# Running the 128-row matmuls of an attention and feed-forward kernel as pairs of 64-row passes, in a new order

## The chip, the cores and the metric

The kernel runs on one core of a Trainium2 chip. The metric is the device time of one execution in microseconds (us).

In the profile PE is TensorE's matmul, PEld its weight load, DVE is VectorE, ACT is ScalarE, POOL is GpSimd and SP is SyncE. To *evict* a bank is to copy a finished result out of it, by ACT or DVE; until then the program writes no new result into it. L328 is a line of the source; nearly all matmuls go through one helper and so have one line.

## The reference

```python
x = A_x                                   # 1 x 2048 x 448
xn = layernorm(x)
# A: 16 query heads, 8 key/value heads of 256, the last 512 keys of the cache
q = (xn @ wq)                             # 448 -> 16 * 256
p = softmax(q @ k.T * 256 ** -0.5)        # 2048 x 512 for each head, no mask
s = (p @ v) @ wo                          # 16 * 256 -> 448
# B
g = silu((gelu(xn @ w_gate) * (xn @ w_up)) @ w_down)    # 448 -> 1792 -> 448
out = x + s * g
```

The queries are taken in four chunks of 512, so attention is 64 (chunk, head) steps. I call such a step a head.

## The kernel before

The query projection and gate/up contract over 448 rows, which is seven times 64. They already run as *pairs*: one matmul on rows 0 to 63 and one on rows 64 to 127, at the same time, into two banks (a bank takes one result of up to 128x512). In a first phase each half of the array feeds one bank; in a second phase they swap banks. A second phase waits until the first has landed (`before`). A *unit* is one head's query projection into one pair of banks.

```python
def group(units, lo, hi, start, stop, phases=(0, 1)):
    ...                                             # cut: loop over phases and units
                for u, j in ((0, ph), (1, 1 - ph)):
                    rows = slice(R * u, R * u + R)  # R = 64
                    ...
            before = [last_row[b][0]] if b in last_row and last_row[b][1] != ph else []
```

The rest runs as full 128-row matmuls. Scores (S) go into four banks AB, P V into two of four banks BB, alternating by head. P V follows two heads behind, because its operand `pT` comes from a DMA transpose of the normalized probabilities `pn`.

```python
def s_mm(m):
    for t4 in range(4):
        b = AB[t4]
        mms([... for e in range(2)], ..., (b_ps[b],))   # two matmuls of 128x512
        # ACT: exp of the bank to p32, with its row sum; DVE: reciprocal, normalize to pn
        # after each second tile: DMA transpose pn -> pT

def pv(m):
    for e in range(2):
        b = BB[m % 2 * 2 + e]
        mms([... for j in range(NJ)], ..., (b_ps[b],))  # four matmuls
        # evict to oT: e == 0 by ACT, e == 1 by DVE

for m in range(NS):
    if m in groups:                                     # heads 0, 8, 20, 32, 44, 56
        for i in range(m, groups[groups.index(m) + 1], 2):
            q_group(i, (cur, nxt)[i // 2 % 2])          # cur is AB, nxt is BB: two units each
        ...
    s_mm(m)
    if m < LAG:                                         # LAG = 2
        down(NQC - LAG + m, nxt)
        ...
    if len(late) == LAG:
        pv(late.pop(0))
    ...                                                 # cut: output projection at the end of a chunk
    late.append(m)
```

A block of query projections and a block of heads alternate. Twelve query slots hold the evicted `qT`, so five query blocks follow the first.

The softmax here doesn't subtract the row's maximum and nothing guards it: scores larger than these inputs give would overflow.

Of the kernel before, what the change touches and what calls it, by code (L numbers as in the profile page):

```python
# [164 lines left out]
def bass_recurrent_scan__sliding_block_cached__geglu_ffn__prompt_kernel(  # L165
# [31 lines left out]
    CUT = D - P  # L197
    HG = 8
    NG = Hq // HG
    QS = 12  # L200

    es = ExitStack()
    with es:
# [3 lines left out]
        def place(name, shape, dt, at=None):  # L207
            size = {BF16: 2, F32: 4}[dt]
            for n in shape[1:]:
                size *= n  # L210
            size = (size + 31) // 32 * 32
            if at is None:
                at = base[0]
                base[0] += size
            assert at + size <= nc.sbuf_usable_end, (name, at + size, nc.sbuf_usable_end)
            return nc.alloc_sbuf_tensor_at(name, list(shape), dt, offset=at), at, at + size

        def sbuf_bufs(at, size, n):
            return [K.buf(at + i * size, size) for i in range(n)]
# [67 lines left out]
        b_gl = sbuf_bufs(a, QC * 2, NGL)  # L287


        NPT, NPN, NP32 = 3, 3, 3  # L290
        pT, a, at = place("pT", [P, NPT, 2, 2, NJ, P], BF16, at=rf)
        b_pT = [sbuf_bufs(a + i * QC * NJ * 2, QC * NJ, 2) for i in range(NPT)]
        pn, a, at = place("pn", [P, NPN, 2, W], BF16, at=at)
        b_pn = sbuf_bufs(a, 2 * W * 2, NPN)
        p32, a, at = place("p32", [P, NP32, W], F32, at=at)
# [1 line left out]
        assert at <= b_wgu.hi  # L297
        oT, a, at = place("oT", [P, NCO, QC], BF16, at=b_wgu.hi)
        b_oT = sbuf_bufs(a, QC * 2, NCO)
        qT, a, at = place("qT", [P, QS, 2, QC], BF16, at=b_gl[0].lo - (QS - HG) * 2 * QC * 2)  # L300
        assert b_oT[-1].hi <= a
        b_qT = [[K.buf(a + (h * 2 + e) * QC * 2, QC * 2) for e in range(2)] for h in range(QS)]

        pall = [es.enter_context(nc.psum_tensor("bank%d" % i, [P, 1024], F32)) for i in range(4)]
        bank = [pall[i // 2][:, (i % 2) * 512:(i % 2) * 512 + 512] for i in range(8)]
# [3 lines left out]
        out_view = out.rearrange("b (t p) d -> p (b t) d", p=P)  # L309

        def qs(n):
            return QS - 1 - n % QS


        def dma(q, o, i, reads=(), writes=()):
# [2 lines left out]
        def dma_t(o, i, reads=(), writes=()):  # L318
            K.op("sp", lambda e, o=o, i=i: e.dma_start_transpose(o, i), reads, writes, dma=True)

        def act(o, i, func, reads, writes, scale=1.0):
            K.op("act", lambda e, o=o, i=i: e.activation(o, i, func, scale=scale), reads, writes)  # L322

        def mms(lst, reads, writes, after=()):
            def fn(e):
                ins = None
                for (o, l, r, st, sp) in lst:
                    ins = e.matmul(o, lhsT=l, rhs=r, start=st, stop=sp)  # L328
                return ins
            return K.op("pe", fn, reads, writes, after=after)  # L330
# [107 lines left out]

        last_row = {}

        def warm(n, b, w):
            def fn(e):
                ins = None
                for i in range(n):
                    ins = e.matmul(bank[b][:, 0:w], lhsT=gl[:, 0, 0:P], rhs=gl[:, 0, 0:w], start=True, stop=True)
                return ins
            last_row[b] = (K.op("pe", fn, (b_gl[0],), b_ps[b:b + 2]), None)
# [39 lines left out]
        def bk(pairs, j):  # L487
            return pairs[j // 2] + j % 2

        def gu_evac(n, b):  # L490
# [3 lines left out]
            K.op("dve", lambda e: e.tensor_tensor(actT[:, c % 2, f, :], bank[b + 1], gl[:, s, :], ALU.mult),  # L494
                 (b_ps[b + 1], b_gl[s]), (b_actT[c % 2][f],))

        def down(c, pairs):
            for t4 in range(4):
                t = c * 4 + t4
                b = bk(pairs, t4)  # L500
                mms([(bank[b][:, 0:D], actT[:, c % 2, f, t4 * P:(t4 + 1) * P], wd[:, f, :], f == 0, f == NF - 1)
                     for f in range(NF)], [b_wd] + b_actT[c % 2], (b_ps[b],))
                s = t % 2
                act(tmp[:, s, :], bank[b][:, 0:D], ACT.Tanh, (b_ps[b],), b_tmp[s], scale=0.5)
                K.op("dve", lambda e, t=t, b=b, s=s: e.scalar_tensor_tensor(
                    out=g2[:, t, :], in0=tmp[:, s, :], scalar=1.0, in1=bank[b][:, 0:D],
                    op0=ALU.add, op1=ALU.mult), b_tmp[s] + [b_ps[b]], (b_g2[t],))

        def ln_first(t):
            ln_stats(t)  # L510
# [23 lines left out]
        ln_first(1)  # L534
        ln_second(0)
        ln_tp_pe(0, ((0, 6), (1, 4)))
        warm(2, 2, QC // 2)
        ln_second(1, "act")
        HEAD, PH = (0, 1, 2), (0, 2, 4)
        T = ((None, 6),)  # L540
# [91 lines left out]

        AB, BB = [], []

        def s_mm(m):
            s, g = qs(m), m % Hq // 2
            for t4 in range(4):
                b = AB[t4]
                mms([(bank[b], qT[:, s, e, t4 * P:(t4 + 1) * P], kT[:, g, e, :], e == 0, e == 1) for e in range(2)],
                    [b_kT[g]] + b_qT[s], (b_ps[b],))  # L640
                n = m * 4 + t4
                r, z, y, x = n % NRS, n % NP32, n // 2 % NPN, n // 4 % NPT
                K.op("act", lambda e, b=b, r=r, z=z: e.activation(  # L643
                    p32[:, z, :], bank[b], ACT.Exp, scale=att_scale, accum_out=rsum[:, r:r + 1]),
                    (b_ps[b],), (b_p32[z], b_rsum[r]))
                K.op("dve", lambda e, r=r: e.reciprocal(rden[:, r:r + 1], rsum[:, r:r + 1]), (b_rsum[r],), (b_rden[r],))  # L646
                K.op("dve", lambda e, r=r, z=z, y=y, t=t4 % 2: e.tensor_scalar(  # L647
                    pn[:, y, t, :], p32[:, z, :], rden[:, r:r + 1], None, op0=ALU.mult),
                    (b_p32[z], b_rden[r]), (b_pn[y],))
                if t4 % 2 == 1:  # L650
                    dma_t(pT[:, x, t4 // 2, :, :, :].rearrange("p t j q -> p (t j) q"),
                          pn[:, y, :, :].rearrange("p t k -> p (t k)"), (b_pn[y],), (b_pT[x][t4 // 2],))

        def pv(m):
            h = m % Hq
            g, x = h // 2, m % NPT
            for e in range(2):
                b = BB[m % 2 * 2 + e]
                mms([(bank[b].rearrange("p (t q) -> p t q", q=P), va[:, g, j, e * P:(e + 1) * P],
                      pT[:, x, :, :, j, :].rearrange("p a t q -> p (a t) q"), j == 0, j == NJ - 1)  # L660
                     for j in range(NJ)], [b_va[g]] + b_pT[x], (b_ps[b],))
                i = 2 * h + e
                if e == 0:
                    act(oT[:, i, :], bank[b], ACT.Copy, (b_ps[b],), (b_oT[i],))
                else:
                    K.op("dve", lambda v, i=i, b=b: v.tensor_copy(oT[:, i, :], bank[b]), (b_ps[b],), (b_oT[i],))  # L666

        def wo_mm(t4, b, lo, hi, c0=0, c1=D):
            ch = list(range(lo, hi))
            mms([(bank[b][:, c0:c1], oT[:, i, t4 * P:(t4 + 1) * P], wo[:, i, c0:c1], i == 0, i == NCO - 1)  # L670
                 for i in ch],
                [b_oT[i] for i in ch] + [b_wo[p] for p in sorted({i // 8 for i in ch})],
                (b_ps[b],))

        def wo_fin(c, t4, b, c0=0, c1=D):
            t = c * 4 + t4
# [10 lines left out]
            if t + NXR < NT:  # L687
                dma("pool", xr[:, t % NXR, :], x_view[:, t + NXR, :], (), (b_xr[t % NXR],))

        LAG = 2  # L690
        late = []
        NS = NQC * Hq
        groups = [0, HG] + list(range(HG + QS, NS, QS)) + [NS]

        act(tmp[:, 1, 0:1], nhalf[:, :], ACT.Exp, (b_nhalf,), (b_tmp[1][0],))
        K.reuse([b for y in b_qT[QS - HG:] for b in y])
        AB.extend(bk(cur, j) for j in range(4))
        BB.extend(bk(nxt, j) for j in range(4))
        for m in range(NS):
            if m in groups:  # L700
                for i in range(m, groups[groups.index(m) + 1], 2):
                    q_group(i, (cur, nxt)[i // 2 % 2])
                if m == 0:
                    K.reuse([b for x in b_pT for b in x] + b_pn + b_p32)
            s_mm(m)
            if m < LAG:
                down(NQC - LAG + m, nxt)
                if m == LAG - 1:
                    K.reuse(b_oT + [b for y in b_qT[:QS - HG] for b in y])
            if len(late) == LAG:  # L710
                pv(late.pop(0))
            if m > Hq and m % Hq == LAG - 1:
                c = m // Hq - 1
                for t4 in range(4):
                    if t4 == 0:
                        wo_mm(0, BB[0], 0, NCO - 2)
                        wo_mm(0, BB[0], NCO - 2, NCO)
                    else:
                        wo_mm(t4, BB[t4], 0, NCO)
                    wo_fin(c, t4, BB[t4])  # L720
            late.append(m)
        c = NQC - 1
        LATE = NCO - 2 * (LAG + 1)
        wo_mm(0, AB[0], 0, LATE)
        pv(late.pop(0))
        pv(late.pop(0))
        wo_mm(1, AB[1], 0, LATE)
        wo_mm(0, AB[0], LATE, NCO)
        wo_fin(c, 0, AB[0])
        wo_mm(1, AB[1], LATE, NCO)  # L730
        wo_fin(c, 1, AB[1])
        wo_mm(2, AB[2], 0, NCO)
        wo_fin(c, 2, AB[2])
        for i in range(2):
            b = (AB[3], BB[0])[i]
            lo, hi = ((0, CUT), (CUT, D))[i]
            wo_mm(3, b, 0, NCO, lo, hi)
            wo_fin(c, 3, b, lo, hi)
# [55 lines left out]
```

## Time and profile before

556.44 us, median of 4 runs (556.19 to 556.74).

| | before |
|---|---|
| PE busy, share of the span | 547.6 us, 99% |
| PE's share of the chain that ended last | 98% |
| start to start, 128x512 full matmul | 216 ns |
| start to start, 64x512 pair | 216 ns |
| start to start, 128x448 full matmul | 189 ns |

From the page: the span, the busy time of each engine, the granted clock in 40 slices (9 is full), and the chain of waits by engine.

```profile
span 554.7 us, 9719 instructions
...
PE 547.6 (99%) x3603; PEld 261.2 (47%) x3628; DVE 317.2 (57%) x817; ACT 273.6 (49%) x727; POOL 32.7 (6%) x64
...
PEclk9999999999999999999999999999999999999999
...
PE 98%; DMA 1%; issue 0%; DVE 0%; SPq 0%; ACT 0%
```

The last column of the groups below is the idle time of the engine just before their instructions. Behind the matmuls of P V and of the queries there is none. The busy time of one matmul (379 or 376 ns) is longer than its start-to-start distance, because matmuls are pipelined; it must not be multiplied by a count.

```profile
L328 PE MATMUL bank<-pT,va 128*128 128x512 bf16 x512 | 120.8, 379 | 0.0
L328 PE MATMUL bank<-kT,qT 128*128 128x512 bf16 x487 | 117.8, 379 | 2.0 <-ACT qT L322 1.0
L328 PE MATMUL bank<-xnT,wq 64*128 64x512 bf16 x768 | 94.4, 376 | 0.0
```

So costs are read from starts. This is the timeline of PE (start, duration, engine, line, tile, number of instructions) at the end of a query block.

```profile
272.43 0.38 PE L328 MATMUL bank<-xnT,wqr 64*128 64x512 bf16 x2
272.65 1.46 PE L328 MATMUL bank<-xnT,wq 64*128 64x512 bf16 x12
274.27 1.67 PE L328 MATMUL bank<-kT,qT 128*128 128x512 bf16 x7 [0.16 <-ACT qT L322]
275.78 1.89 PE L328 MATMUL bank<-pT,va 128*128 128x512 bf16 x8
277.50 1.89 PE L328 MATMUL bank<-kT,qT 128*128 128x512 bf16 x8
279.23 1.89 PE L328 MATMUL bank<-pT,va 128*128 128x512 bf16 x8
```

One pair takes 272.65 - 272.43 = 0.22 us. Eight full matmuls take 279.23 - 277.50 = 1.73 us, 0.216 each. (Of the first score block one record is missing, "x7".) And this is a start of a query block:

```profile
253.98 1.89 PE L328 MATMUL bank<-pT,va 128*128 128x512 bf16 x8
255.80 0.82 PE L328 MATMUL bank<-xnT,wq 64*128 64x512 bf16 x6
```

Here eight full matmuls take 1.82 us to the next start, not 1.73: 0.1 us is lost between full matmuls and pairs. The Trainium skill, "TensorEngine Tiling (Array Packing)", section Tiling Modes, says that changing the tiling mode drains the TensorE. The trace shows the loss, not the drain itself: about 0.09 to 0.11 us at each of 15 such edges (six from queries to scores, five from P V to queries, four around the down projections), 1.5 us in all. At the six edges from queries to scores the first score matmul has no record ("x7" above; 487 records stand beside 512 weight loads), so there one distance of 216 ns is taken off as well.

### The profile page before, as it was taken

To read this page: it belongs to the slowest core of one execution; us is meant where nothing else is said; L and a number is where in the kernel's file an instruction comes from. 1 tells how busy PE (TensorE), PEld (TensorE's weight loads), DVE (VectorE), ACT (ScalarE), POOL (GpSimd) and SP (SyncE) were. 2 spreads that over 40 slices of the span, in tenths; PEclk is the share of its full clock that TensorE was granted. 3 is DMA by queue.
4 is the path that set the end of the run, shared out by engine and by line. 5 is a ranking of instruction groups with operands and counts; after the bars stand their busy time and mean duration, and the time that the engine had idled before them with its cause. 6 is when DMAs were issued, how large, how long until landed. Compare 5 with 4: busy or idle time off the path is not lost.

```text
span 554.7 us, 9719 instructions
## 1 busy us (share of the span) xinstructions
PE 547.6 (99%) x3603; PEld 261.2 (47%) x3628; DVE 317.2 (57%) x817; ACT 273.6 (49%) x727; POOL 32.7 (6%) x64
## 2 busy tenths in 40 slices
PE   8999999999999999999999999999999999999997
PEld 5554444444544444554444444544444454444455
DVE  6673734443385588326588745258747625858722
ACT  5432324353485588205588635058747505758600
POOL 1120580000000000000000000000000000000000
PEclk9999999999999999999999999999999999999999
DMA  9540399901156077413086803157704713618601
GB/s 295 115 141 9 79 302 307 213 1 39 38 134 96 5 149 157 88 35 92 1 153 152 153 1 77 33 94 164 146 11 95 134 34 90 153 19 153 153 8 34
DMA packets 163599, 57.63 MB, mean 104 GB/s; under 512 B 151456, under 2 KB 160672, under 8 KB 163552
## 3 DMA queue, kind: packets, MB, share of 16 engines
q1 hardware_dynamic: 159488, 45.16, 38.8%
q0 software_dynamic: 3296, 11.27, 6.7%
q8 instruction: 29, 0.48, 0.4%
q10 hardware_dynamic: 768, 0.57, 0.3%
q14 instruction: 18, 0.15, 0.1%
HBM read 17.92 MB, written 1.84 MB: 36 GB/s over the span
## 4 chain that ended last, share of the span: by engine, by line
PE 98%; DMA 1%; issue 0%; DVE 0%; SPq 0%; ACT 0%
PE bank L328 98%; DMA x<-in_A_x_dram 1%; SPq L316 0%; DVE stats L375 0%; ACT xnT L322 0%; DVE tmp L681 0%; ACT ve L391 0%; DVE ofin L684 0%; PE bank L426 0%; DVE mv L378 0%
## 5 line engine op out<-in xcount | busy, mean ns | idle before, releaser
L643 ACT ACTIVATE p<-bank 128x512 f32<-128x512 f32 x256 | 149.2, 597 | 103.3 <-PE bank L328 101.4
L647 DVE TENSOR_SCALAR pn<-p,rden 128x512 bf16<-128x512 f32 x256 | 124.6, 487 | 14.4 <-DMA pT<-pn 5.4
L328 PE MATMUL bank<-pT,va 128*128 128x512 bf16 x512 | 120.8, 379 | 0.0
L328 PE MATMUL bank<-kT,qT 128*128 128x512 bf16 x487 | 117.8, 379 | 2.0 <-ACT qT L322 1.0
L328 PE MATMUL bank<-wo,oT 128*128 128x448 bf16 (+2 forms) x544 | 97.7, 341 | 0.0
L328 PE MATMUL bank<-xnT,wq 64*128 64x512 bf16 x768 | 94.4, 376 | 0.0
L328 PE MATMUL bank<-xnT,wgu 64*128 64x512 bf16 (+2 forms) x768 | 83.9, 350 | 0.4 <-ACT xnT L322 0.4
L328 PEld LDWEIGHTS bank<-pT,va 128*128 128x128 bf16 x512 | 50.1, 98 | 60.4 <-DMA pT<-pn 0.2
L328 PEld LDWEIGHTS bank<-kT,qT 128*128 128x128 bf16 x512 | 49.6, 98 | 61.3 <-issue 2.5
L328 PEld LDWEIGHTS bank<-wo,oT 128*128 128x128 bf16 x544 | 52.0, 98 | 45.5
L630 DVE CAST qT<-bank 128x512 bf16<-128x512 f32 x64 | 42.9, 692 | 51.9 <-PE bank L328 51.9
L322 ACT ACTIVATE qT<-bank 128x512 bf16<-128x512 f32 x64 | 38.2, 597 | 60.7 <-PE bank L328 59.1
L328 PEld LDWEIGHTS bank<-xnT,wq 64*128 64x128 bf16 x768 | 36.9, 94 | 46.5 <-ACT p L643 2.1
L322 ACT ACTIVATE gl<-bank 128x512 bf16<-128x512 f32 x56 | 33.2, 597 | 49.4 <-PE bank L328 46.2
L494 DVE TENSOR_TENSOR actT<-bank,gl 128x512 bf16<-128x512 f32 x56 | 37.8, 689 | 33.4 <-PE bank L328 26.6
L328 PEld LDWEIGHTS bank<-xnT,wgu 64*128 64x128 bf16 x768 | 36.9, 94 | 37.4 <-issue 0.7
L643 ACT ACTIVATION_READ_ACCUMULATOR p<-bank 128x1 f32 x256 | 52.8, 206 | 0.0
L646 DVE RECIPROCAL rden<-rsum 128x1 f32<-128x1 f32 x256 | 40.4, 158 | 20.6 <-ACT p L643 20.0
L681 DVE SCALAR_TENSOR_TENSOR tmp<-bank,g 128x448 f32<-128x448 f32 (+2 forms) x17 | 10.1, 597 | 72.5 <-PE bank L328 72.5
L666 DVE CAST oT<-bank 128x512 bf16<-128x512 f32 x64 | 43.8, 684 | 6.9 <-PE bank L328 6.9
L328 PE MATMUL bank<-wd,actT 128*128 128x448 bf16 x224 | 43.0, 353 | 0.0
L322 ACT ACTIVATE oT<-bank 128x512 bf16<-128x512 f32 x64 | 39.1, 611 | 7.0 <-PE bank L328 7.0
(39 smaller groups left out, 182.9 us busy)
## 6 DMA issues: line engine op xcount, KB each, us to landing
wo<-in_A_wo_dram POOLq DMA_DIRECT2D x4, 896.0 KB, 19.0
wq<-in_A_wq_dram POOLq DMA_DIRECT2D x2, 1536.0 KB, 10.0
va<-in_A_v_cache_dram POOLq DMA_DIRECT2D x8, 256.0 KB, 13.9
pT<-pn SPq DMA_TRANSPOSE x128, 2.8
xr<-in_A_x_dram POOLq DMA_DIRECT2D x16, 112.0 KB, 2.3
out_dram<-ofin SPq DMA_DIRECT2D x15, 112.0 KB, 1.7
wd<-in_B_w_down_dram SPq DMA_DIRECT2D x1, 1568.0 KB, 7.6
x<-in_A_x_dram SPq DMA_DIRECT2D x2, 448.0 KB, 4.4
```

The source lines that it names most:

```text
L322: K.op("act", lambda e, o=o, i=i: e.activation(o, i, func, scale=scale), reads, writes)
L328: ins = e.matmul(o, lhsT=l, rhs=r, start=st, stop=sp)
L494: K.op("dve", lambda e: e.tensor_tensor(actT[:, c % 2, f, :], bank[b + 1], gl[:, s, :], ALU.mult), (b_ps[b + 1], b_gl[s]), (b_actT[c % 2][ ...
L630: K.op("dve", lambda v, s=s, b=b: v.tensor_copy(qT[:, s, 1, :], bank[b + 1]), (b_ps[b + 1],), (b_qT[s][1],))
L643: K.op("act", lambda e, b=b, r=r, z=z: e.activation(p32[:, z, :], bank[b], ACT.Exp, scale=att_scale, accum_out=rsum[:, r:r + 1]), (b_ps[b] ...
L646: K.op("dve", lambda e, r=r: e.reciprocal(rden[:, r:r + 1], rsum[:, r:r + 1]), (b_rsum[r],), (b_rden[r],))
L647: K.op("dve", lambda e, r=r, z=z, y=y, t=t4 % 2: e.tensor_scalar(pn[:, y, t, :], p32[:, z, :], rden[:, r:r + 1], None, op0=ALU.mult), (b_p ...
L666: K.op("dve", lambda v, i=i, b=b: v.tensor_copy(oT[:, i, :], bank[b]), (b_ps[b],), (b_oT[i],))
L681: K.op("dve", lambda e: e.scalar_tensor_tensor(out=tmp[:, s, c0:c1], in0=bank[b][:, c0:c1], scalar=0.5, in1=g2[:, t, c0:c1], op0=ALU.mult, ...
```

## The change

The intent: with all large products in 64-row pairs, TensorE needn't change its mode. A second phase must wait for the first, so other work has to stand between the two; scores of one head and P V of another are interleaved for that. P V then goes three heads behind, which needs a fourth `pT` buffer; its memory comes from four of the twelve query slots. The core of the diff:

```diff
-    QS = 12
...
-        NPT, NPN, NP32 = 3, 3, 3
+        NPT, NPN, NP32 = 4, 3, 3
...
-        def s_mm(m):
+        def s_mm(m, i, ph):
...
+            b = AB[2 * i]
+            o = mms([(bank[b + v], qT[rows, s, e, (2 * i + v) * P:(2 * i + v + 1) * P], kT[rows, g, e, :],
+                      ph == 0 and e == 0, ph == 1 and e == 1) for e in range(2) for rows, v in HV[ph]],
+                    [b_kT[g]] + b_qT[s], b_ps[b:b + 2], [first["s", i]] if ph else [])
...
-        LAG = 2
+        LAG = 3
...
-            if m in groups:
-                for i in range(m, groups[groups.index(m) + 1], 2):
-                    q_group(i, (cur, nxt)[i // 2 % 2])
+            if m % HG == 0:
+                for i in range(0, HG, 2):
+                    q_group(m + i, (cur, nxt)[i // 2 % 2])
...
-            s_mm(m)
...
+                p = late.pop(0)
+                s_mm(m, 0, 0)
+                pv(p, 0)
+                s_mm(m, 0, 1)
+                s_mm(m, 1, 0)
+                pv(p, 1)
+                s_mm(m, 1, 1)
```

Cut: the same treatment of `pv`, `down` and the output projection, a warm-up in pairs, and a new order at the very end, where the last output tiles stay full matmuls.

More of the change, by code (lines that the diff above doesn't have):

```diff
@@ L287, in bass_recurrent_scan__sliding_block_cached__geglu_ffn__prompt_kernel, with place_pT @@
         b_gl = sbuf_bufs(a, QC * 2, NGL)
-        NPT, NPN, NP32 = 3, 3, 3
-        pT, a, at = place("pT", [P, NPT, 2, 2, NJ, P], BF16, at=rf)
-        b_pT = [sbuf_bufs(a + i * QC * NJ * 2, QC * NJ, 2) for i in range(NPT)]
+        NPT, NPN, NP32 = 4, 3, 3
+        pT = [None] * NPT
+        b_pT = [None] * NPT
+        at = rf
+        def place_pT(i, at):
+            pT[i], a, at = place("pT%d" % i, [P, 2, 2, NJ, P], BF16, at=at)
+            b_pT[i] = sbuf_bufs(a, QC * NJ, 2)
+            return at
+        for i in range(NPT - 1):
+            at = place_pT(i, at)
         pn, a, at = place("pn", [P, NPN, 2, W], BF16, at=at)
@@ L299, in bass_recurrent_scan__sliding_block_cached__geglu_ffn__prompt_kernel @@
         b_oT = sbuf_bufs(a, QC * 2, NCO)
-        qT, a, at = place("qT", [P, QS, 2, QC], BF16, at=b_gl[0].lo - (QS - HG) * 2 * QC * 2)
-        assert b_oT[-1].hi <= a
-        b_qT = [[K.buf(a + (h * 2 + e) * QC * 2, QC * 2) for e in range(2)] for h in range(QS)]
+        at = place_pT(NPT - 1, at)
+        assert at <= b_gl[0].lo
+        qT, a, at = place("qT", [P, HG, 2, QC], BF16, at=b_gl[0].lo)
+        b_qT = [[K.buf(a + (h * 2 + e) * QC * 2, QC * 2) for e in range(2)] for h in range(HG)]
         pall = [es.enter_context(nc.psum_tensor("bank%d" % i, [P, 1024], F32)) for i in range(4)]
@@ L311, in qs @@
         def qs(n):
-            return QS - 1 - n % QS
+            return HG - 1 - n % HG
         def dma(q, o, i, reads=(), writes=()):
@@ L439, in bass_recurrent_scan__sliding_block_cached__geglu_ffn__prompt_kernel, with warm_pairs, fn @@
         last_row = {}
+        def warm_pairs(n, b, w):
+            def fn(e):
+                ins = None
+                for i in range(n):
+                    for u in range(2):
+                        r = slice(R * u, R * u + R)
+                        ins = e.matmul(bank[b + u][:, 0:w], lhsT=gl[r, 0, 0:P], rhs=gl[r, 0, 0:w], start=True, stop=True)
+                return ins
+            last_row[b] = (K.op("pe", fn, (b_gl[0],), b_ps[b:b + 2], after=[last_row[b][0]]), None)
         def warm(n, b, w):
@@ L495, in gu_evac, with halves @@
                  (b_ps[b + 1], b_gl[s]), (b_actT[c % 2][f],))
+        def halves():
+            return [[(slice(R * u, R * u + R), u ^ ph) for u in range(2)] for ph in range(2)]
+        HV = halves()
         def down(c, pairs):
-            for t4 in range(4):
-                t = c * 4 + t4
-                b = bk(pairs, t4)
-                mms([(bank[b][:, 0:D], actT[:, c % 2, f, t4 * P:(t4 + 1) * P], wd[:, f, :], f == 0, f == NF - 1)
-                     for f in range(NF)], [b_wd] + b_actT[c % 2], (b_ps[b],))
-                s = t % 2
-                act(tmp[:, s, :], bank[b][:, 0:D], ACT.Tanh, (b_ps[b],), b_tmp[s], scale=0.5)
-                K.op("dve", lambda e, t=t, b=b, s=s: e.scalar_tensor_tensor(
-                    out=g2[:, t, :], in0=tmp[:, s, :], scalar=1.0, in1=bank[b][:, 0:D],
-                    op0=ALU.add, op1=ALU.mult), b_tmp[s] + [b_ps[b]], (b_g2[t],))
+            first = [None, None]
+            for ph in range(2):
+                for i in range(2):
+                    b = pairs[i]
+                    o = mms([(bank[b + v][:, 0:D], actT[rows, c % 2, f, (2 * i + v) * P:(2 * i + v + 1) * P],
+                              wd[rows, f, :], ph == 0 and f == 0, ph == 1 and f == NF - 1)
+                             for f in range(NF) for rows, v in HV[ph]],
+                            [b_wd] + b_actT[c % 2], b_ps[b:b + 2], first[i:i + 1] if ph else [])
+                    first[i] = o
+                    for v in range(2 * ph):
+                        t = c * 4 + 2 * i + v
+                        s = t % 2
+                        act(tmp[:, s, :], bank[b + v][:, 0:D], ACT.Tanh, (b_ps[b + v],), b_tmp[s], scale=0.5)
+                        K.op("dve", lambda e, t=t, b=b + v, s=s: e.scalar_tensor_tensor(
+                            out=g2[:, t, :], in0=tmp[:, s, :], scalar=1.0, in1=bank[b][:, 0:D],
+                            op0=ALU.add, op1=ALU.mult), b_tmp[s] + [b_ps[b + v]], (b_g2[t],))
         def ln_first(t):
@@ L536, in bass_recurrent_scan__sliding_block_cached__geglu_ffn__prompt_kernel @@
         ln_tp_pe(0, ((0, 6), (1, 4)))
-        warm(2, 2, QC // 2)
+        warm_pairs(2, 2, QC // 2)
         ln_second(1, "act")
@@ L633, in bass_recurrent_scan__sliding_block_cached__geglu_ffn__prompt_kernel @@
         AB, BB = [], []
-        def s_mm(m):
+        first = {}
+        def s_mm(m, i, ph):
             s, g = qs(m), m % Hq // 2
-            for t4 in range(4):
-                b = AB[t4]
-                mms([(bank[b], qT[:, s, e, t4 * P:(t4 + 1) * P], kT[:, g, e, :], e == 0, e == 1) for e in range(2)],
-                    [b_kT[g]] + b_qT[s], (b_ps[b],))
-                n = m * 4 + t4
-                r, z, y, x = n % NRS, n % NP32, n // 2 % NPN, n // 4 % NPT
-                K.op("act", lambda e, b=b, r=r, z=z: e.activation(
+            b = AB[2 * i]
+            o = mms([(bank[b + v], qT[rows, s, e, (2 * i + v) * P:(2 * i + v + 1) * P], kT[rows, g, e, :],
+                      ph == 0 and e == 0, ph == 1 and e == 1) for e in range(2) for rows, v in HV[ph]],
+                    [b_kT[g]] + b_qT[s], b_ps[b:b + 2], [first["s", i]] if ph else [])
+            first["s", i] = o
+            if ph == 0:
+                return
+            y, x = (2 * m + i) % NPN, m % NPT
+            for v in range(2):
+                n = m * 4 + 2 * i + v
+                r, z = n % NRS, n % NP32
+                K.op("act", lambda e, b=b + v, r=r, z=z: e.activation(
@@ L644, in s_mm @@
                     p32[:, z, :], bank[b], ACT.Exp, scale=att_scale, accum_out=rsum[:, r:r + 1]),
-                    (b_ps[b],), (b_p32[z], b_rsum[r]))
+                    (b_ps[b + v],), (b_p32[z], b_rsum[r]))
                 K.op("dve", lambda e, r=r: e.reciprocal(rden[:, r:r + 1], rsum[:, r:r + 1]), (b_rsum[r],), (b_rden[r],))
-                K.op("dve", lambda e, r=r, z=z, y=y, t=t4 % 2: e.tensor_scalar(
-                    pn[:, y, t, :], p32[:, z, :], rden[:, r:r + 1], None, op0=ALU.mult),
+                K.op("dve", lambda e, r=r, z=z, v=v: e.tensor_scalar(
+                    pn[:, y, v, :], p32[:, z, :], rden[:, r:r + 1], None, op0=ALU.mult),
@@ L649, in s_mm, with pv @@
                     (b_p32[z], b_rden[r]), (b_pn[y],))
-                if t4 % 2 == 1:
-                    dma_t(pT[:, x, t4 // 2, :, :, :].rearrange("p t j q -> p (t j) q"),
-                          pn[:, y, :, :].rearrange("p t k -> p (t k)"), (b_pn[y],), (b_pT[x][t4 // 2],))
-        def pv(m):
+            dma_t(pT[x][:, i, :, :, :].rearrange("p t j q -> p (t j) q"),
+                  pn[:, y, :, :].rearrange("p t k -> p (t k)"), (b_pn[y],), (b_pT[x][i],))
+        def pv(m, ph):
             h = m % Hq
@@ L656, in pv @@
             g, x = h // 2, m % NPT
-            for e in range(2):
-                b = BB[m % 2 * 2 + e]
-                mms([(bank[b].rearrange("p (t q) -> p t q", q=P), va[:, g, j, e * P:(e + 1) * P],
-                      pT[:, x, :, :, j, :].rearrange("p a t q -> p (a t) q"), j == 0, j == NJ - 1)
-                     for j in range(NJ)], [b_va[g]] + b_pT[x], (b_ps[b],))
-                i = 2 * h + e
-                if e == 0:
-                    act(oT[:, i, :], bank[b], ACT.Copy, (b_ps[b],), (b_oT[i],))
-                else:
-                    K.op("dve", lambda v, i=i, b=b: v.tensor_copy(oT[:, i, :], bank[b]), (b_ps[b],), (b_oT[i],))
+            b = BB[m % 2 * 2]
@@ new lines, in pv @@
+            o = mms([(bank[b + v].rearrange("p (t q) -> p t q", q=P), va[rows, g, j, v * P:(v + 1) * P],
+                      pT[x][rows, :, :, j, :].rearrange("p a t q -> p (a t) q"), ph == 0 and j == 0,
+                      ph == 1 and j == NJ - 1) for j in range(NJ) for rows, v in HV[ph]],
+                    [b_va[g]] + b_pT[x], b_ps[b:b + 2], [first["p", m % 2]] if ph else [])
+            first["p", m % 2] = o
+            if ph == 0:
+                return
+            i = 2 * h
+            act(oT[:, i, :], bank[b], ACT.Copy, (b_ps[b],), (b_oT[i],))
@@ new lines, in pv, with wo_reads, wo_pair @@
+            K.op("dve", lambda v: v.tensor_copy(oT[:, i + 1, :], bank[b + 1]), (b_ps[b + 1],), (b_oT[i + 1],))
+        def wo_reads(ch):
+            return [b_oT[i] for i in ch] + [b_wo[p] for p in sorted({i // 8 for i in ch})]
+        def wo_pair(k, b, ph, lo, hi):
+            ch = list(range(lo, hi))
+            o = mms([(bank[b + v][:, 0:D], oT[rows, i, (2 * k + v) * P:(2 * k + v + 1) * P], wo[rows, i, :],
+                      ph == 0 and i == 0, ph == 1 and i == NCO - 1) for i in ch for rows, v in HV[ph]],
+                    wo_reads(ch), b_ps[b:b + 2], [first["w", k]] if ph else [])
+            if ph == 0:
+                first["w", k] = o
@@ L670, in wo_mm @@
             mms([(bank[b][:, c0:c1], oT[:, i, t4 * P:(t4 + 1) * P], wo[:, i, c0:c1], i == 0, i == NCO - 1)
-                 for i in ch],
-                [b_oT[i] for i in ch] + [b_wo[p] for p in sorted({i // 8 for i in ch})],
-                (b_ps[b],))
+                 for i in ch], wo_reads(ch), (b_ps[b],))
         def wo_fin(c, t4, b, c0=0, c1=D):
@@ L688, in wo_fin @@
                 dma("pool", xr[:, t % NXR, :], x_view[:, t + NXR, :], (), (b_xr[t % NXR],))
-        LAG = 2
+        LAG = 3
         late = []
         NS = NQC * Hq
-        groups = [0, HG] + list(range(HG + QS, NS, QS)) + [NS]
         act(tmp[:, 1, 0:1], nhalf[:, :], ACT.Exp, (b_nhalf,), (b_tmp[1][0],))
-        K.reuse([b for y in b_qT[QS - HG:] for b in y])
+        K.reuse([b for y in b_qT for b in y])
         AB.extend(bk(cur, j) for j in range(4))
@@ L699, in bass_recurrent_scan__sliding_block_cached__geglu_ffn__prompt_kernel @@
         for m in range(NS):
-            if m in groups:
-                for i in range(m, groups[groups.index(m) + 1], 2):
-                    q_group(i, (cur, nxt)[i // 2 % 2])
+            if m % HG == 0:
+                for i in range(0, HG, 2):
+                    q_group(m + i, (cur, nxt)[i // 2 % 2])
                 if m == 0:
-                    K.reuse([b for x in b_pT for b in x] + b_pn + b_p32)
-            s_mm(m)
-            if m < LAG:
-                down(NQC - LAG + m, nxt)
-                if m == LAG - 1:
-                    K.reuse(b_oT + [b for y in b_qT[:QS - HG] for b in y])
@@ L710, in bass_recurrent_scan__sliding_block_cached__geglu_ffn__prompt_kernel @@
-            if len(late) == LAG:
-                pv(late.pop(0))
+                    K.reuse([b for x in b_pT[:NPT - 1] for b in x] + b_pn + b_p32)
+            if len(late) == LAG:
+                p = late.pop(0)
[5 more added lines that the diff above has]
+                s_mm(m, 1, 1)
+            else:
+                for ph in range(2):
+                    s_mm(m, 0, ph)
+                    s_mm(m, 1, ph)
@@ L712, in bass_recurrent_scan__sliding_block_cached__geglu_ffn__prompt_kernel @@
+            late.append(m)
+            if m < 2:
+                down(NQC - 2 + m, nxt)
+                if m == 1:
+                    K.reuse(b_oT + b_pT[NPT - 1])
             if m > Hq and m % Hq == LAG - 1:
                 c = m // Hq - 1
-                for t4 in range(4):
-                    if t4 == 0:
-                        wo_mm(0, BB[0], 0, NCO - 2)
-                        wo_mm(0, BB[0], NCO - 2, NCO)
-                    else:
-                        wo_mm(t4, BB[t4], 0, NCO)
-                    wo_fin(c, t4, BB[t4])
@@ L721, in bass_recurrent_scan__sliding_block_cached__geglu_ffn__prompt_kernel @@
-            late.append(m)
+                wo_pair(0, BB[0], 0, 0, NCO - 2)
+                wo_pair(0, BB[0], 0, NCO - 2, NCO)
+                wo_pair(1, BB[2], 0, 0, NCO)
+                for k in range(2):
+                    wo_pair(k, BB[2 * k], 1, 0, NCO)
+                    for v in range(2):
+                        wo_fin(c, 2 * k + v, BB[2 * k + v])
         c = NQC - 1
         LATE = NCO - 2 * (LAG + 1)
-        wo_mm(0, AB[0], 0, LATE)
-        pv(late.pop(0))
-        pv(late.pop(0))
@@ L727, in bass_recurrent_scan__sliding_block_cached__geglu_ffn__prompt_kernel @@
-        wo_mm(1, AB[1], 0, LATE)
-        wo_mm(0, AB[0], LATE, NCO)
-        wo_fin(c, 0, AB[0])
-        wo_mm(1, AB[1], LATE, NCO)
-        wo_fin(c, 1, AB[1])
-        wo_mm(2, AB[2], 0, NCO)
+        wo_pair(0, AB[0], 0, 0, LATE)
+        pv(late[0], 0)
+        pv(late[1], 0)
+        pv(late[0], 1)
+        pv(late[1], 1)
+        wo_pair(0, AB[0], 1, 0, LATE - 4)
+        pv(late[2], 0)
+        wo_pair(0, AB[0], 1, LATE - 4, LATE)
+        pv(late[2], 1)
+        wo_mm(2, AB[2], 0, NCO - 2)
@@ L733, in bass_recurrent_scan__sliding_block_cached__geglu_ffn__prompt_kernel @@
+        wo_mm(2, AB[2], NCO - 2, NCO)
         wo_fin(c, 2, AB[2])
+        for t4 in (1, 0):
+            wo_mm(t4, AB[t4], LATE, NCO)
+            wo_fin(c, t4, AB[t4])
         for i in range(2):
```

## The prediction

> **Bound now.** TensorE. Part 1 of the page gives PE 547.6 us of a 554.7 us span, the chain of waits is 98% PE, the clock is full in every slice. The timeline shows the issue rate: eight 128-row score matmuls (512 columns) take 1.73 us to the next block's start, 216 ns each; nine 64-row pairs of the query projection take 1.94 us, also 216 ns a pair. Output-projection matmuls (448 columns) start 189 ns apart. A pair costs what one 128-row matmul costs, and as many columns are streamed before and after: the arithmetic gains nothing. Weight loads don't limit pairs: 128-column pairs in the head start 56 ns apart.
>
> **Removed.** Only changes of tiling mode. The Trainium skill, "TensorEngine Tiling (Array Packing)", Tiling Modes, says that a mode change drains the TensorE. This trace agrees and gives the size: a P V block followed by query pairs takes 1.82 us to the next start instead of 1.73, about 0.1 us; the down projection's edges show the same. About 15 such edges: gain 1.5 us, all critical. Nothing here can give 2%.
>
> **Added.** New order per head: S0a, PVa, S0b, S1a, PVb, S1b (0.43, 0.86, 0.43, 0.43, 0.86, 0.43 us). Two score tiles now finish at the very end of a head, with nothing behind them that leaves their banks alone.
>
> From the timeline: an eviction starts about 0.21 us after its pair's stream ends; exponentials follow each other every 0.57 us; one ends 0.69 us after its start with its accumulator read; the PE starts about 0.06 us after a releaser's end.
>
> 1. Start of a query block (7 times: heads 8 to 56). Its second unit needs the banks of the last two score tiles 0.86 us after the scores end; their second exponential ends at about 1.55 us (a P V eviction is ahead of it). Before, a 1.73 us P V stood between. Stall 0.7 us x 7 = 5 us.
> 2. End of a query block (7 times). P V of an odd head comes 0.43 us after the last query pair and needs exactly the last unit's banks, whose VectorE eviction (0.69 us) ends at 0.9 us. Before, 1.73 us of scores stood between. Stall 0.5 us x 7 = 3.6 us.
> 3. Head 3 follows head 2 without P V: 1.1 us, once.
> 4. Steady heads: the last exponential ends 1.55 to 1.6 us after the scores' end; its bank is wanted at 1.73. Slack 0.1 us, where it was over 1. Waits of pn for its transpose (six in the waits view, up to 1.1 us) now reach the PE: 0 to 5 us, 1.5 expected.
>
> ScalarE and VectorE work is unchanged, 2.8 and 3.1 us per 3.45 us head.
>
> **Sum.** 556.7 - 1.5 + 5 + 3.6 + 1.1 + 1.5 = 566.4 us, range 560.5 to 571.0. Chances: faster by over 2%: 0.01; within 2%: 0.67; slower by over 2% (above 567.8): 0.32.
>
> **What would show it.** Pairs at 216 and 189 ns; edges of 0.1 us gone; in the waits view, PE waiting for ACT p about seven times for 0.7 us and for DVE qT about seven times for 0.5 us; PE share about 97%. If 4 is right, short PE waits for ACT p within a query group.
>
> **What would make it wrong.** Steady heads that stall each time (0.1 us x 55): up to 572. Pairs faster than 216 ns would make it a gain; nothing in this trace shows that. If the waits at block edges are hidden: 555.

## The result, and the profile after

564.46 us, median of 4 runs (564.43 to 564.63): 8.0 us more. The ratio is 1.014, with a 95% interval of 1.0122 to 1.0158. Ratios in this document need not be the ratio of the medians quoted (here 1.0144).

The page of the changed kernel, same lines:

```profile
span 562.7 us, 12926 instructions
...
PE 550.9 (98%) x5310; PEld 269.3 (48%) x5310; DVE 316.2 (56%) x817; ACT 278.7 (50%) x727; POOL 32.7 (6%) x64
...
PEclk9999999999999999999999999999999999999999
...
PE 93%; ACT 4%; DVE 2%; issue 0%; ACTq 0%
```

PE's share of the chain falls from 98% to 93%, and ACT and DVE enter it. The chain in order of time (start, length, what) shows where; these are the pieces around the first query block after the start:

```profile
152.93 17.03 PE bank L336 x156
170.00 0.47 issue
170.47 1.27 ACT p L681 x4
171.79 10.77 PE bank L336 x98
182.58 1.35 DVE qT L660 x2
183.97 25.66 PE bank L336 x236
```

An exponential (`p`) holds up the start of the block, an eviction of the queries (`qT`) its end. The waits view (who waited for whom: us in total, times, longest) gives the counts:

```profile
PE bank L336 <- ACT p L681: 4.8, 8, 0.9
...
PE bank L336 <- DVE qT L660: 2.5, 7, 0.4
```

The timeline at 170 us, PE and ACT lines:

```profile
169.78 0.59 PE L336 MATMUL bank<-kT,qT 64*128 64x512 bf16 x4
169.98 0.60 ACT L330 ACTIVATE oT<-bank 128x512 bf16<-128x512 f32 x1
...
170.21 0.81 PE L336 MATMUL bank<-xnT,wq 64*128 64x512 bf16 x6
170.47 0.59 ACT L681 ACTIVATE p<-bank 128x512 f32<-128x512 f32 x1
...
170.85 0.38 PE L336 MATMUL bank<-xnT,wqr 64*128 64x512 bf16 x2
...
171.04 0.60 ACT L681 ACTIVATE p<-bank 128x512 f32<-128x512 f32 x1
...
171.52 0.21 ACT L681 ACTIVATION_READ_ACCUMULATOR p<-bank 128x1 f32 x1
171.78 0.33 PEld L336 LDWEIGHTS bank<-xnT,wq 64*128 64x128 bf16 x6 [1.05 <-ACT p L681]
171.79 0.60 PE L336 MATMUL bank<-xnT,wq 64*128 64x512 bf16 x4 [0.55 <-ACT p L681]
```

The last scores of head 7 start at 169.78, the first unit of the query block at 170.21. The second unit would start at 171.07, but its banks hold the last two score tiles. ACT first evicts a P V result, then takes the two exponentials, and the second one's accumulator read ends at 171.73. The unit starts at 171.79: 0.72 us lost.

The view says 0.55 us of idle, because a matmul counts as busy for 376 ns although the next one of the same size can start 216 ns later. The loss is idle time plus 0.16 us. The end of the same block, PE and DVE lines:

```profile
181.72 1.46 PE L336 MATMUL bank<-xnT,wq 64*128 64x512 bf16 x12
...
182.58 1.34 DVE L660 CAST qT<-bank 128x512 bf16<-128x512 f32 x2 [1.68 <-PE bank L336]
...
183.02 0.60 PE L336 MATMUL bank<-kT,qT 64*128 64x512 bf16 x4
183.97 0.55 PEld L336 LDWEIGHTS bank<-pT,va 64*128 64x128 bf16 x8 [0.85 <-DVE qT L660]
183.97 0.82 PE L336 MATMUL bank<-pT,va 64*128 64x512 bf16 x6 [0.36 <-DVE qT L660]
```

P V could start at 183.45, 0.43 us after the scores. It needs the banks of the last query unit, whose eviction ends at 183.92: 0.36 + 0.16 = 0.52 us lost. A bank evicted at one place in the program is wanted too soon at another.

Added up from the matmul starts in the traces (a start later than 216 or 189 ns after the one before, less that distance; the second matmul of a pair starts 4 ns after the first, so a loss counted from it comes out up to 4 ns too small):

| term | before | after |
|---|---|---|
| changes of mode | 15, 1.5 us | 1 (near the end), 0.1 us |
| start of a query block | 0 | 7, 5.0 us |
| end of a query block | 0 (but the mode) | 7, 3.6 us |
| head 3 after head 2 | 0 | 1, 1.1 us |
| other waits among the heads | 0 | 1, 0.1 us |

The difference is -1.5 + 0.1 + 5.0 + 3.6 + 1.1 + 0.1 = 8.4 us, for 8.0 us measured between the spans. The rest stands mostly outside these terms, at the start of the run: the first 512-column pair starts at 11.35 us, before the change at 11.70. In the other runs with the new start it comes at 11.25 to 11.62, and in e6_slots8, with the old one, at 11.57, so this part is not shown to be the change's doing. From the first query matmul to the last matmul, the traces differ by 446.0 - 436.9 = 9.1 us.

### The profile page after: what moved, and what is told of

It is laid out like the page before. It is cut to its first block, busy times and chain, and to the rows that moved or that the text cites. A ratio compares the mean times of both kernels' runs of the same rounds, so it can differ in the third digit from the quotient of the medians.

```text
span 562.7 us, 12926 instructions
## 1 busy us (share of the span) xinstructions
PE 550.9 (98%) x5310; PEld 269.3 (48%) x5310; DVE 316.2 (56%) x817; ACT 278.7 (50%) x727; POOL 32.7 (6%) x64
## 4 chain that ended last, share of the span: by engine, by line
PE 93%; ACT 4%; DVE 2%; issue 0%; ACTq 0%
PE bank L336 93%; ACT p L681 3%; DVE qT L660 2%; PE bank L463 1%; ACT oT L330 0%; PE bank L434 0%; ACT xnT L330 0%; DVE tmp L730 0%; DVE ofin L733 0%; DVE gl L366 0%; ACTq L151 0%; DVE epst L367 0%
## 5 line engine op out<-in xcount | busy, mean ns | idle before, releaser
L336 PE MATMUL bank<-kT,qT 64*128 64x512 bf16 x1024 | 133.0, 376 | 0.9 <-ACT p L681 0.9
L336 PE MATMUL bank<-pT,va 64*128 64x512 bf16 x1024 | 131.0, 376 | 2.5 <-DVE qT L660 2.5
L336 PE MATMUL bank<-wo,oT 64*128 64x448 bf16 (+3 forms) x976 | 98.1, 343 | 0.0
L336 PEld LDWEIGHTS bank<-pT,va 64*128 64x128 bf16 x1024 | 49.3, 94 | 64.8 <-DVE qT L660 6.0
L336 PEld LDWEIGHTS bank<-kT,qT 64*128 64x128 bf16 x1024 | 49.8, 94 | 61.7 <-ACT p L681 17.6
L336 PEld LDWEIGHTS bank<-wo,oT 64*128 64x128 bf16 (+1 forms) x976 | 51.6, 94 | 46.0 <-issue 0.7
L336 PEld LDWEIGHTS bank<-xnT,wgu 64*128 64x128 bf16 x768 | 40.7, 94 | 33.0 <-ACT xnT L330 0.3
L681 ACT ACTIVATION_READ_ACCUMULATOR p<-bank 128x1 f32 x256 | 51.2, 200 | 0.0
L336 PE MATMUL bank<-wd,actT 64*128 64x448 bf16 x448 | 43.1, 349 | 0.0
```

The lines of the kernel that those rows point to most:

```text
L336: ins = e.matmul(o, lhsT=l, rhs=r, start=st, stop=sp)
L681: K.op("act", lambda e, b=b + v, r=r, z=z: e.activation(p32[:, z, :], bank[b], ACT.Exp, scale=att_scale, accum_out=rsum[:, r:r + 1]), (b_p ...
```

## The experiments

The theory: pairs cost exactly what full matmuls cost; a change of mode costs 0.1 us; the time comes from banks that are wanted too soon at the edges of the query blocks and at head 3. Rival A: the pairs themselves cost, with twice the matmuls and weight loads. Rival B: eight query slots, and so more query blocks, cost.

### e1_banks: other banks for the query units

```diff
-                    q_group(m + i, (cur, nxt)[i // 2 % 2])
+                    q_group(m + i, (cur, nxt)[i // 2 % 2] if m == 0 else
+                            ((cur[0], nxt[1]), (cur[1], nxt[0]))[i // 2 % 2])
```

Each pair of units now takes one score pair and one P V pair of banks, so chosen that none was used a moment before and none is wanted a moment after.

> Changed kernel; only the banks of the query units are paired otherwise from head 8 on: (first score pair, second P V pair), then (second score pair, first P V pair). Same instructions, same pairs, same 8 slots. Theory (waits for banks at both edges of seven query blocks): both waits vanish, 7 x (0.72 + 0.52) = 8.7 us less, 564.5 to about 555.8 us, slightly under the kernel before. Rival A (the 64-row pairs themselves cost, twice the weight loads): stays at 564. Rival B (eight slots instead of twelve cost by their number of blocks): stays near 564 as well, since seven blocks remain.

Measured: 555.56 us (5 runs), beside 556.39 for the kernel before; ratio 0.9986 (0.9973 to 0.9999). In its trace no query block has a late start at either edge. The chain of waits is 99% PE again, and these are all the waits of PE's matmuls through the helper (the first is head 3, the second comes before the queries):

```profile
PE 99%; ACT 0%; DVE 0%; issue 0%
...
PE bank L336 <- ACT p L681: 0.9, 1, 0.9
...
PE bank L336 <- ACT xnT L330: 0.2, 1, 0.2
```

The instructions are those of the changed kernel, 5310 matmuls and seven blocks, with the same eight slots, four `pT` buffers and P V three heads behind, so rivals A and B both fall as the cause of the 8 us. The change in the place of a bank is worth 8.9 us by the medians; the late starts that are gone from the trace add up to 8.7 us.

### e2_start and e3_end: one edge each

```diff
 # e2_start
+ ... (cur, nxt)[i // 2 % 2] if m == 0 or i >= 4 else ((cur[0], nxt[1]), (cur[1], nxt[0]))[i // 2 % 2]
 # e3_end
+ ... (cur, nxt)[i // 2 % 2] if m == 0 or i < 6 else (nxt[1], nxt[0])
```

> Changed kernel; only the first two units pairs of a query block take the other banks, so only the wait at the start of a block should go. Theory: 7 x 0.72 = 5.0 us less, about 559.4 us; PE waiting for DVE qT stays at seven times 0.52 us. Rivals: 564.

> Changed kernel; only the last query unit pair of a block is taken in reversed order, so that the banks which P V needs next are evicted first. Theory: only the wait at the end of a block goes, 7 x 0.52 = 3.6 us less, about 560.8 us; PE waiting for ACT p at block starts stays. Rivals: 564.

Measured: 559.47 us and 561.30 us (4 runs each), as expected within 0.5 us. (The diffs above are shortened; the call is the same as in e1_banks.) In e2_start the waits at the block ends are all that is left of the seven-fold ones:

```profile
PE bank L336 <- DVE qT L660: 2.5, 7, 0.4
...
PE bank L336 <- ACT p L681: 1.3, 2, 0.9
```

In e3_end PE's matmuls never wait for qT, but nine times for p, 5.4 us in all. The two edges are separate and add up: 5.0 us and 3.2 us alone, 8.9 us together. The 0.7 us that the sum lacks has a visible part: each of the two has one further wait among the heads, 0.50 and 0.64 us, against 0.13 us in the changed kernel and in e1_banks.

### e6_slots8: the kernel before with eight slots

```diff
-    QS = 12
+    QS = 8
-        groups = [0, HG] + list(range(HG + QS, NS, QS)) + [NS]
+        groups = [0, HG] + list(range(2 * HG, NS, QS)) + [NS]
```

> Kernel before with eight query slots instead of twelve, 128-row matmuls and the old order kept: seven query blocks after the first instead of five. Theory: two more blocks, each with two mode changes of 0.1 us: plus 0.4 us, about 556.8 us. Rival B (the smaller number of slots made most of the loss): about 560 us or more.

Measured: 557.01 us (5 runs), beside 556.39; ratio 1.001 (0.9996 to 1.0024). The medians differ by 0.6 us, near the 0.4 expected, and the interval includes none at all. Its trace has the four more changes of mode, 0.4 us. Two more blocks by themselves cost next to nothing. In the changed kernel they matter only because each block brings 1.24 us of waits.

### e5_pv128: P V as full matmuls again, on top of e1_banks

```diff
 # shortened; the first of the two P V tiles is now also evicted earlier, after its own four matmuls
-            b = BB[m % 2 * 2]
-            o = mms([(bank[b + v]..., va[rows, g, j, v * P:(v + 1) * P], pT[x][rows, :, :, j, :]..., ...)
-                     for j in range(NJ) for rows, v in HV[ph]], ...)
+            b = BB[m % 2 * 2] + ph
+            mms([(bank[b]..., va[:, g, j, ph * P:(ph + 1) * P], pT[x][:, :, :, j, :]..., j == 0, j == NJ - 1)
+                 for j in range(NJ)], [b_va[g]] + b_pT[x], (b_ps[b],))
```

> As e1_banks, but P V as full 128-row matmuls again, in the same two places of each head: four changes between 64-row and 128-row mode per head, 244 in 61 heads and a few at the end. Theory (a mode change costs 0.095 to 0.106 us, a pair as much as a full matmul): about plus 24 us over e1_banks, near 580 us, with PE starts 312 and 319 ns apart at the edges instead of 212 and 216. Rival A (pairs cost more than full matmuls): the P V part gets cheaper and the time falls or rises by far less than 24 us.

Measured: 581.80 us (4 runs), 26.2 us more than e1_banks. PE's timeline in e5_pv128:

```profile
197.49 1.04 PE L336 MATMUL bank<-kT,qT 64*128 64x512 bf16 x8
198.46 1.04 PE L336 MATMUL bank<-pT,va 128*128 128x512 bf16 x4
199.43 1.04 PE L336 MATMUL bank<-kT,qT 64*128 64x512 bf16 x8
```

And at the same place in e1_banks:

```profile
197.54 1.03 PE L336 MATMUL bank<-kT,qT 64*128 64x512 bf16 x8
198.40 1.03 PE L336 MATMUL bank<-pT,va 64*128 64x512 bf16 x8
199.26 1.03 PE L336 MATMUL bank<-kT,qT 64*128 64x512 bf16 x8
```

Four pairs or four full matmuls take 0.86 us without a change of mode and 0.97 us with one. The starts show 0.095 us at each change to pairs and 0.092 us at each change to full matmuls (the 4 ns of the count; from the first matmul of the pair it is 0.096 us); the second start after a change is another 0.011 us late. There are 244 changes in the 61 heads and 5 at the end, 248 more than in e1_banks, which makes about 0.106 us a change. Apart from head 3 the trace has no other late start. The mechanism that the change was meant to remove is real; the kernel before just had few of these edges.

### e4_order: the interleaving undone

```diff
                 s_mm(m, 0, 0)
-                pv(p, 0)
-                s_mm(m, 0, 1)
                 s_mm(m, 1, 0)
-                pv(p, 1)
+                s_mm(m, 0, 1)
                 s_mm(m, 1, 1)
+                pv(p, 0)
+                pv(p, 1)
```

> Changed kernel with the interleaving alone undone: all four score blocks of a head, then both P V phases. Theory: the waits at both edges of the query blocks go (minus 8.7 us), since 1.73 us of other work again stands between; but the second P V phase then waits for the first to land, about 0.27 us in each of 61 heads, plus 16.5 us: about 572 us. Rival A: no waits at the edges lost, 564 or more by the self-waits alone, 581.

Measured: 571.18 us (4 runs). Both waits at the block edges are gone, and PE waits for itself:

```profile
PEld bank L336 <- PE bank L336: 34.3, 63, 0.6
```

The matmul starts show 0.225 us between the two P V phases in each of 61 heads, 13.7 us in all; I had estimated 0.27. The next start is another 0.011 us late each time, 0.7 us together. Head 3 has a second wait, 0.7 us, which I had not foreseen. With the 8.7 us of the edges gone that sums to 6.4 us, or 6.6 with the 4 ns of the count, for 6.7 us measured over the changed kernel. So the interleaving is needed, and saves more than the edges cost; what was missing was another choice of banks to go with it.

### e7_all: head 3 too

```diff
             if m == 0:
                 q_group(0, cur)
                 q_group(2, nxt)
                 ...
             elif m % HG == 0:
                 ...                                  # as in e1_banks
             ...                                      # scores of head m, P V of an earlier head
+            if m == 0:
+                q_group(4, nxt)
+                q_group(6, (cur[1], nxt[0]))
-            if m < 2:
-                down(NQC - 2 + m, nxt)
-                if m == 1:
+            if m in (1, 2):
+                down(NQC - 3 + m, nxt)
+                if m == 2:
```

> As e1_banks, and the wait of head 3 taken away as well: head 0's scores go between the query units of the first block, and the two late down projections follow heads 1 and 2, so that no two heads' scores stand side by side without other work. Theory: 1.1 us less than e1_banks, about 554.7 us, that is 1.5 to 1.8 us under the kernel before, the worth of its mode changes. Rival A: no gain over the kernel before.

Measured: 555.09 us (5 runs), beside 556.33; ratio 0.9979 (0.9966 to 0.9991). Against e1_banks this is 0.5 us less, where 1.1 was expected. It was run at another time.

### e8_head3, e9_banks and e10_all: head 3 alone, and the two best side by side

e8_head3 has the edit of e7_all in the changed kernel without the other banks; e9_banks and e10_all are e1_banks and e7_all again, on one chip.

> Changed kernel; only the order around the first heads is altered, so that head 3's scores don't follow head 2's with nothing between; the waits at the edges of the later query blocks stay. Theory: 564.5 less 1.1 us, about 563.4 us; the one PE wait of 1.09 us gone. If the first run of e7_all (0.5 us less than e1_banks in separate calls) is the true size, about 564.0.

> The same kernel as e1_banks, again, to stand on one chip beside the next one: 555.6 us.

> The same kernel as e7_all, again, beside e9_banks: by the trace of the first runs 0.7 to 0.9 us less than e9_banks, about 554.8 us; if the first medians are right, 0.5 us less.

Measured: 563.79 us (4 runs), 555.63 us and 555.02 us (5 runs each). The first is 0.7 us less than the changed kernel's median, the third 0.6 us less than the second. All three comparisons (0.5, 0.7 and 0.6 us) give about half of the expectation. In both traces the wait of 1.09 us is gone. From the first query matmul to the last matmul, the stretch shrinks by 0.89 us in e8_head3 (446.00 to 445.11); two new waits of 0.14 us each stand among later heads. From the last matmul to the end of the run the trace has 0.18 us more (3.56 against 3.38 us), in both kernels with this edit. What lengthens this tail is open; no run here was made for it. The traces show only two values of it: 3.4 us in the changed kernel, e1_banks, e2_start, e3_end, e5_pv128 and e9_banks, 3.6 us in the kernel before, e4_order, e6_slots8 and all runs with the edit of head 3. Small late starts also come and go between runs of one program: e9_banks has one of 0.13 us at the start of a query block that e1_banks has not.

e10_all is the fastest version: 555.02 us beside 556.47 for the kernel before, ratio 0.9975 (0.9963 to 0.9988). That is about what the 14 removed changes of mode are worth, but partly by chance: in its trace the removed changes save 1.4 us, two new waits among the heads cost 0.3 us, and the first 512-column pair starts 0.45 us earlier than in the kernel before (11.25 against 11.70), a time that varies from run to run.

## Why the prediction was right or wrong

The prediction was 566.4 us with a range of 560.5 to 571.0; the time is 564.46. The class (within 2%) held as well. Of the 1.9 us between them, 1.4 are step 4 and 0.3 the starting figure (556.7 where the median was 556.44).

| step of the prediction | predicted | shown |
|---|---|---|
| pairs at the rate of full matmuls | 216 and 189 ns | 216 and 189 ns; e5_pv128 shows both forms at 0.86 us for four |
| changes of mode removed | -1.5 us | -1.4 us by the starts; e10_all is 1.4 us under the kernel before, in part by chance (see there) |
| 1. start of a query block | 7 x 0.7 = 5 us | 7 x 0.72 = 5.0 us; e2_start is 5.0 us faster |
| 2. end of a query block | 7 x 0.5 = 3.6 us | 7 x 0.52 = 3.6 us; e3_end is 3.2 us faster |
| 3. head 3 | 1.1 us | 1.09 us in the trace; removing it gives 0.6 to 0.7 us |
| 4. steady heads | 1.5 us, 0 to 5 | 0.1 us |

- **The bound and the main mechanism were right.** TensorE was saturated, the arithmetic of pairs gains nothing, and the only thing to win was 1.5 us.
- **Steps 1 and 2 were right in place, count and size.** They came from three durations in the trace of the kernel before (exponential pitch 0.57 us, DVE eviction 0.69 us, 0.21 us until an eviction starts) and from reading which bank each piece of the new order wants.
- **Step 4 was mis-sized.** I expected delays of the transposes to reach the PE now and then, 1.5 us in all. They do occur: DVE's pn waits for its transpose 11 times, 5.9 us in all. But only one short PE wait of 0.13 us shows among the steady heads, at 521.20 us. It follows such a wait: at 517.89 pn had waited 0.80 us, and the read that frees the bank ends at 521.14. By the waits view ACT's exponentials waited for DVE only twice (once for pn, once for `rden`, 0.5 us each), so most of these delays do not reach even ACT. And the slack in front of PE is larger than I had worked out:

```profile
193.69 0.60 ACT L330 ACTIVATE oT<-bank 128x512 bf16<-128x512 f32 x1
194.18 0.59 ACT L681 ACTIVATE p<-bank 128x512 f32<-128x512 f32 x1
...
194.75 0.60 ACT L681 ACTIVATE p<-bank 128x512 f32<-128x512 f32 x1
194.78 0.60 PE L336 MATMUL bank<-pT,va 64*128 64x512 bf16 x4
...
195.21 1.03 PE L336 MATMUL bank<-kT,qT 64*128 64x512 bf16 x8
195.22 0.21 ACT L681 ACTIVATION_READ_ACCUMULATOR p<-bank 128x1 f32 x1
```

In this steady head of the changed kernel the last exponential's read ends at 195.43 us. Its bank is wanted by the second half of the eight score matmuls, at 195.21 + 0.43 = 195.64. That is 0.2 us, not 0.1: ACT begins the next exponential sooner after a P V eviction than after another exponential (194.18 - 193.69 = 0.49 us, where I had used 0.57). How much of the missing 1.4 us each of these two explains is not shown: no run was made for step 4.

- **One sign was off.** I wrote that PE's share of the span would fall to about 97%; the page has 98%. The busy count runs on for 0.16 us into each wait, so it understates the loss. PE's share of the chain, 98% to 93%, shows it more plainly.

## What to carry to other kernels

Before changing the order of work on a saturated engine, list for each edge between stages which buffer the first piece of the next stage wants, and when its last reader is done; here this gave the two large terms, 8.6 us, from durations of the old trace alone. Interleaving two streams puts the end of both at the very end of a step, and so takes away the distance that used to hide evictions; the repair was not another order but another assignment of banks, one line. Count the edges before removing a cost per edge: 0.1 us each is worth 26 us at 248 added edges and 1.5 us at 15.

## What the Trainium skill lacked or had wrong

- "TensorEngine Tiling (Array Packing)", Tiling Modes, says that a change of tiling mode drains the TensorE, but gives no size. The runs show about 0.09 to 0.11 us at the edge, and about 0.106 us a change in all when 248 of them are added (26.2 us).
- "TensorE: Matmul & The Clock Gate", Back-to-back issue gap, gives a sustained distance of about 131 ns for 512 columns and about 81 ns for 128 columns in streams of weight loads and matmuls, and calls 216 ns the isolated case. Long streams with a weight load for every matmul keep 216 ns at 512 columns, and 56 ns at 128 (the output projection's last 32 matmuls). The point is about the figures of that section alone.
- Neither of these two pages gives the cost of waiting in a second 64-row phase for the first to land: 0.225 us between 512-column phases with nothing between, and another 0.011 us at the next start (e4_order).
